# A transformer block on one core: QKV and output projections in 64-row tile pairs, one PSUM pool of six banks, the FFN gate applied to the sums, searched scheduler priorities

## The chip, the cores and the metric

The kernel runs on one core of a Trainium2 chip. The metric is the device time of one execution in microseconds (us); the "span" of a profile runs from the first to the last recorded instruction and is about 1.8 us shorter. The engines are named as the profile names them: PE (TensorE, matmuls), PEld (its weight loads, which overlap with PE), DVE (VectorE), ACT (ScalarE), POOL (GpSimd) and SP (SyncE, which here issues most of the transfers). A line number such as L614 is a line of the kernel that was profiled, so the same step has other numbers in the changed kernel. A "tile" of PE below is the part of the 128x128 array that a matmul uses: all 128 rows, or 64, or 28 to 32 of them, and all columns or 64 or 32 of them; the tile mode is this size. PSUM holds the sums that matmuls write; the kernel divides it into banks of 512 float32 columns. An eviction is the operation that reads a finished sum out of a bank, and only after it is the bank free again.

## The reference

One block with adaptive layer norm, for 2048 tokens of 448 numbers in bfloat16. The attention is local and dilated: each token looks at eight keys, 0, 2, ..., 14 positions back.

```python
# cut to what matters; S = 2048, D = 448, H = 16 heads of 28, F = 1792, dtype bfloat16
mod = silu(c) @ w_mod                       # six vectors of 448: sa, ca, ga, sb, cb, gb
h = layernorm(x) * (1 + ca) + sa
q, k, v = split(h @ wqkv)                   # wqkv: 448 x 1344
o = softmax(q . k[t - 0, 2, ..., 14] / sqrt(28)) @ v      # per head
x = x + ga * (o @ wo)
h = layernorm(x) * (1 + cb) + sb
gate, up = h @ W_gate, h @ W_up             # 448 x 1792 each
x = x + gb * ((relu(gate) * up) @ W_down)
```

The contraction over D = 448 matters here: it is three and a half times 128, and exactly seven times 64.

## The kernel before

The kernel hands every operation to a static scheduler in Python. It knows for each operation an engine (or several), an estimated duration, a priority and what it depends on. It orders the operations on each engine, assigns PSUM banks and buffers, and derives the semaphore waits. An order on an engine is therefore decided by priorities and by estimates, not by the order of the program text.

```python
class _Plan:
    def op(self, eng, cost, fn, r=(), w=(), prio=0, drain=0.0, dma=0, issue=450.0, mode=128, after=()):
        ...     # `mode` is the tile shape on PE: a change costs SWITCH in the plan's estimate;
        ...     # `after`: PE operations that this one must wait for with a semaphore

psF = es.enter_context(nc.psum_tensor("psF", [128, 4, 512], F32))
psL = es.enter_context(nc.psum_tensor("psL", [128, 2, 512], F32))
psM = es.enter_context(nc.psum_tensor("psM", [128, 2, 512], F32))
poolF = _Slots([psF[:, i, :] for i in range(4)])      # QK, V, gate/up
poolL = _Slots([psL])                                 # scores
poolM = _Slots([psM[:, i, :] for i in range(2)])      # denominators, attention sums, projection, down

def stage_qk(b, prio):                                # per block b of 512 tokens
    for g in range(4):
        for sec in range(2):                          # q, then k
            buf = _Buf(poolF)
            def mm(e, g=g, sec=sec, buf=buf):
                for k in range(4):                    # rows 448..511 are zeros
                    last = e.matmul(buf.at, Wqk[:, k, 512 * sec + 128 * g:512 * sec + 128 * g + 128],
                                    hT[:, k, KOFF + TB * b:KOFF + TB * b + TB], start=(k == 0), stop=(k == 3))
                return last
            ...   # evictions to qT (twice, with alternate heads zeroed) or kT

def stage_v(t, prio):                                 # per attention tile t of 114 tokens (18 tiles)
    ...
    for k in range(4):
        last = e.matmul(buf.at[0:nk, 0:D], hT[:, k, KOFF + k0:KOFF + k0 + nk], Wv[:, k, :],
                        start=(k == 0), stop=(k == 3))

def stage_y(j, prio, eprio):                          # output projection, 128 tokens, mode 128
    ...
    for g in range(4):                                # four groups of 4 heads x 32 rows (28 used)
        last = e.matmul(buf.at[:, 0:D], qT[:, g, s0:s0 + 128], wo_pad[:, g, :], start=(g == 0), stop=(g == 3))

def stage_gu(b, h2, prio, eprio):                     # gate and up side by side in 64-row tiles, mode 64
    ...
    for c in range(7):
        e.matmul(bufs[0].at, Wgu[0:64, c, 128*f:128*f+128], h2.at[0:64, kg, :], start=(c == 0), stop=(c == 6))
        e.matmul(bufs[1].at, Wgu[64:128, c, 128*f:128*f+128], h2.at[64:128, ku, :], start=(c == 0), stop=(c == 6))

# the gate gb (gbc[:, 1]) is multiplied into W_down, once:
for f in range(NF):                                   # NF = 14
    op(POOL, 1000, lambda e, f=f: e.tensor_tensor(Wd[:, f, :], Wd[:, f, :], gbc[:, 1, :], ALU.mult),
       r=[("Wd", f), ("gbc", 1)], w=[("Wds", f)], prio=900)
# ... so that a down projection ends with one addition:
op(DVE, 620, lambda e, ...: e.tensor_tensor(o.at, buf.at[:, 0:D], x_sb[:, t, :], ALU.add), ...)
```

The down projection runs in 64-row pairs in two of the four blocks (`DN64 = (1, 2)`) and in 128 rows in the others. Score matmuls use 64 rows; denominators and attention sums use all rows and 32 columns.

The softmax here doesn't subtract the row's maximum and nothing guards it: scores larger than these inputs give would overflow.

Of the kernel before, what the change touches and what calls it, by code (L numbers as in the profile page):

```python
# [5 lines left out]
ACT = mybir.ActivationFunctionType  # L6
# [19 lines left out]
DNP = (1350, 1550, 1750, 1950)  # L26
# [25 lines left out]
class _Plan:  # L52
# [3 lines left out]
    DMA_NS_PER_BYTE = 1.0 / 240.0  # L56
# [7 lines left out]
    def op(self, eng, cost, fn, r=(), w=(), prio=0, drain=0.0, dma=0, issue=450.0, mode=128, after=()):  # L64
# [22 lines left out]
        else:  # L87
            alts = [(e, float(c), f) for e, c, f in eng]
        self.ops.append(dict(id=oid, alts=alts, deps=deps, allocs=allocs, prio=prio,
                             drain=drain, dma=dma, issue=issue, mode=mode, after=list(after)))  # L90
# [7 lines left out]
    def schedule(self):  # L98
# [14 lines left out]
        mode = 128  # L113
        slack = {PE: 30.0 + self.SWITCH, ACTE: 60.0, DVE: 60.0, POOL: 60.0, SP: 60.0}
# [22 lines left out]
        for _ in range(n):  # L137
            cands = {e: [] for e in ENGINES}
            for oid in avail:
# [14 lines left out]
                for a, (e, c, f) in enumerate(o["alts"]):  # L154
# [10 lines left out]
                    st = max(free[e] + (self.SWITCH if e == PE and o["mode"] != mode else 0.0), rt)  # L165
                    if best is None or st + c < best[0] - 1e-6:
                        best = (st + c, st, a, e)
# [22 lines left out]
            if o["dma"]:  # L190
                free[e] = st + o["issue"]
                b0 = max(free[e], dma_free)
                dma_free = b0 + o["dma"] * self.DMA_NS_PER_BYTE
                finish[oid] = dma_free + self.DMA_FIXED
            else:
                free[e] = st + cost
                finish[oid] = free[e] + o["drain"]
            o["st"] = st
# [88 lines left out]
def bass_adaLN_cond__sliding_local_dilated__glu_gated_reglu__prompt_kernel(  # L287
# [15 lines left out]
    with ExitStack() as es:  # L303
# [51 lines left out]
        qsc = sb("qsc", [128, 2], F32)  # L355

        psF = es.enter_context(nc.psum_tensor("psF", [128, 4, 512], F32))
        psL = es.enter_context(nc.psum_tensor("psL", [128, 2, 512], F32))
        psM = es.enter_context(nc.psum_tensor("psM", [128, 2, 512], F32))
        poolF = _Slots([psF[:, i, :] for i in range(4)])  # L360
        poolL = _Slots([psL])
        poolM = _Slots([psM[:, i, :] for i in range(2)])
# [20 lines left out]
        op(DVE, 60, lambda e: e.memset(qsc[:], 0.0), w=["qsc"], prio=-15)  # L383
        for r in range(4):
# [4 lines left out]
        op(DVE, 500, lambda e: e.memset(hT[64:128, 3, KOFF:KOFF + 2 * TB], 0.0), w=["hT0"], prio=-13)  # L389
        op(DVE, 500, lambda e: e.memset(Wqk[64:128, 3, :], 0.0), w=["wqkz"], prio=-14)  # L390
        op(DVE, 250, lambda e: e.memset(Wv[64:128, 3, :], 0.0), w=["wvz"], prio=-13)
# [33 lines left out]
        def load_x(ta, tb, prio, eng=SP):  # L425
            load(x_sb[:, ta:tb, :], x2d[128 * ta:128 * tb, :].rearrange("(t p) d -> p t d", p=128),
                 [("x", t) for t in range(ta, tb)], 128 * (tb - ta) * D * 2, prio, eng=eng)

        wmod_v = w_mod.rearrange("(p k) n -> p k n", k=4)
        load(crow[:], c.rearrange("o (p k) -> (o p) k", k=4), ["crow"], 4096, -10)  # L430
        load_x(0, 2, -9)
        load_x(2, 4, -9, eng=ACTE)
        load(wmod[0:112, 0:2, 0:2 * D], wmod_v[:, 0:2, 0:2 * D], ["wmodA0"], D * D * 2, -8)
        load(wmod[0:112, 2:4, 0:2 * D], wmod_v[:, 2:4, 0:2 * D], ["wmodA1"], D * D * 2, -8)
        load(Wv[:, 0:3, :], A_wqkv[0:384, 2 * D:3 * D].rearrange("(k p) n -> p k n", p=128),
             [("wv", k) for k in range(3)], 384 * D * 2, -7)
        load(Wv[0:64, 3, :], A_wqkv[384:448, 2 * D:3 * D], [("wv", 3)], 64 * D * 2, -7)
        load(Wraw[:, 0:3, :], A_wqkv[0:384, 0:2 * D].rearrange("(k p) n -> p k n", p=128),
             [("wraw", k) for k in range(3)], 384 * 2 * D * 2, -7)
        load(Wraw[0:64, 3, :], A_wqkv[384:448, 0:2 * D], [("wraw", 3)], 64 * 2 * D * 2, -7)  # L440
# [13 lines left out]
        op(POOL, 900, lambda e: e.memset(Wqk_h[:, :, :, DH:32], 0.0), r=["wqkz"], w=["wqk0"], prio=-16)  # L454
        for k in range(4):
            for sec in range(2):
                op(DVE, 275, lambda e, k=k, sec=sec: e.tensor_copy(
                    Wqk_h[0:ROWS[k], k, 16 * sec:16 * sec + 16, 0:DH],
                    Wraw[0:ROWS[k], k, D * sec:D * sec + D].rearrange("p (h d) -> p h d", d=DH)),
                   r=[("wraw", k), "wqk0"], w=[("wqk", k, sec)], prio=1)  # L460
# [10 lines left out]
        def mod_cols(vecs, wname, col, prio):  # L471
            buf = _Buf(poolM)

            def mm(e, ks):
                last = None
                for k in ks:
                    for cc in range(4):
                        for vi, vec in enumerate(vecs):
                            M = ROWS[cc]
                            last = e.matmul(buf.at[0:M, 4 * vi + cc:4 * vi + cc + 1],  # L480
                                            wmod[0:112, k, D * vec + 128 * cc:D * vec + 128 * cc + M],
                                            silu[:, k:k + 1], start=(k == 0 and cc == 0 and vi == 0),
# [4 lines left out]
            for i in range(2):  # L487
                op(PE, 750, lambda e, i=i: mm(e, (2 * i, 2 * i + 1)), r=[wname + str(i), "silu"], w=[buf, ("mm", col, i)], prio=prio,
# [23 lines left out]
        def ln_stats(t, stt, mvt, tag, prio, extra=()):  # L512
            op(DVE, 600, lambda e: e.bn_stats(stt[:, t, :], x_sb[:, t, :]), r=[("x", t)] + list(extra),  # L513
               w=[(tag, "st", t)], prio=prio)
            op(DVE, 165, lambda e: e.bn_aggr(mvt[:, t, :], stt[:, t, :]), r=[(tag, "st", t)],
               w=[(tag, "mv", t)], prio=prio)

        def ln_rstd(t0, t1, mvt, lt, rt, nt, tag, prio):
# [5 lines left out]
            op(DVE, 90, lambda e: e.scalar_tensor_tensor(nt[:, t0:t1], mvt[:, t0:t1, 0], -1.0, rt[:, t0:t1],  # L524
# [4 lines left out]
        def ln_normalize(t, rt, nt, tag, prio, eng, extra=()):  # L529
# [3 lines left out]
            op(eng, 390 if eng == DVE else 720, f, r=[("x", t), (tag, "rstd", t), (tag, "nmr", t)], w=[buf] + list(extra),  # L533
               prio=prio)
# [6 lines left out]
        def ln_affine(dst, deps, w, col, rows, cc, prio):  # L541
# [4 lines left out]
            op(POOL, 850, f, r=deps + [("mod", col), ("mod", col + 4)], w=w, prio=prio)  # L546


# [398 lines left out]
```

## Time and profile before

| | before |
|---|---|
| median of the first three runs, known before the prediction | 237.11 us (234.69 to 238.84) |
| median of four, with the one beside the changed kernel | 236.38 us |
| medians in three later sets of 7, 7 and 9 runs on other chips | 235.11, 235.04, 234.87 us |
| the profiled run: time, span, mean granted clock | 234.78 us, 233.0 us, 0.997 |

Below, everything read from profiles is compared with profiles.

The head of the profile page gives the span, and per engine busy time, share and number of instructions:

```profile
span 233.0 us, 5200 instructions
PE 223.9 (96%) x2216; PEld 104.9 (45%) x2216; DVE 148.3 (64%) x291; ACT 124.4 (53%) x212; POOL 60.8 (26%) x83
```

PE is busy for 96% of the span, and the next engine is far behind. The page's groups of instructions show the work in question: line, engine, operation, output<-inputs, tile of the array, size, count | busy us, mean ns | idle before, and what ended it:

```profile
L614 PE MATMUL psF<-hT,Wqk 128*128 128x512 bf16 x128 | 29.3, 380 | 1.4 <-DVE kT L632 1.4
...
L647 PE MATMUL psF<-Wv,hT 128*128 128x448 bf16 (+1 forms) x72 | 15.2, 353 | 1.6 <-ACT hT L575 1.6
...
L860 POOL TENSOR_TENSOR Wd<-Wd,gbc 128x448 bf16<-128x448 bf16 x14 | 14.0, 1031 | 6.3 <-DVE gbc L508 6.3
...
L742 PE MATMUL psM<-wo_pad,qT 128*128 128x448 bf16 x64 | 14.9, 355 | 0.0
```

A mean of 380 ns for a matmul is not its cost: matmuls overlap in the records, and what counts is the distance from one start to the next. The next lines are from the timeline of PE (start, duration, line, operation, count of a group):

```profile
12.60 2.44 PE L647 MATMUL psF<-Wv,hT 128*128 128x448 bf16 x12 [0.89 <-ACT hT L575]
14.88 7.07 PE L614 MATMUL psF<-hT,Wqk 128*128 128x512 bf16 x32
...
118.49 0.38 PE L780 MATMUL psF<-h2T,Wgu 64*128 64x512 bf16 x1
118.49 0.38 PE L782 MATMUL psF<-h2T,Wgu 64*128 64x512 bf16 x1
118.80 0.93 PE L742 MATMUL psM<-wo_pad,qT 128*128 128x448 bf16 x4
119.66 0.38 PE L710 MATMUL psM<-EA,ones 128*32 128x456 bf16 x4
119.97 0.22 PE L682 MATMUL psL<-qT,kT 64*128 64x114 bf16 x2
```

Thirty-two 512-column matmuls take 7.07 us, 0.216 us each, and the two of a 64-row pair start together and also take 0.216 us. Four projection matmuls of 448 columns should take 4 x 0.189 = 0.76 us, but the next work starts 0.86 us after them. The extra 0.1 us appears at each change of the tile mode shown here: gate/up (64 rows) to projection (128 rows), 0.31 us from start to start instead of 0.216; projection to denominators (32 columns), 0.86 instead of 0.76. Few other delays exist. The list of PE's waits shows them (what waited, releaser, total us, times, longest); the line left out is the warm-up before any real work:

```profile
PE psF L647 <- ACT hT L575: 1.6, 2, 0.9
PE psF L614 <- DVE kT L632: 1.4, 1, 1.4
...
PE psL L682 <- ACT EA L694: 0.5, 1, 0.5
```

The end is short: the last matmul's record ends at 229.21 us, then comes one eviction, here from the timeline of DVE, and the last output transfer.

```profile
229.25 0.62 DVE L838 TENSOR_TENSOR o_sb<-psF,x_sb 128x448 bf16<-128x448 f32 x1 [2.03 <-PE psF L831]
```

### The profile page before, as it was taken

The numbers are of one execution on the slowest core, as the hardware profiler recorded it, in microseconds if no ns is written. First come the engines' busy times: TensorE is split into PE (matmuls) and PEld (weight loads), VectorE is DVE, ScalarE is ACT, GpSimd is POOL, SyncE is SP. The second block draws the span as 40 slices with busy tenths as digits, with TensorE's granted clock in tenths as the row PEclk, the third lists the DMA queues.
The fourth block names the chain that finished last, engine by engine and source line by source line (L and its number), as shares of the span: only waits on it lengthen the run. The fifth ranks groups of instructions, "written<-read, shape, count | busy, mean of one in ns | idle before, by whom it ended". The sixth has DMA issues, their size and how long they took to land. (4 is left out here: it accounts for less than half of the span.)

```text
span 233.0 us, 5200 instructions
## 1 busy us (share of the span) xinstructions
PE 223.9 (96%) x2216; PEld 104.9 (45%) x2216; DVE 148.3 (64%) x291; ACT 124.4 (53%) x212; POOL 60.8 (26%) x83
## 2 busy tenths in 40 slices
PE   7989899999997999999999999999999999999993
PEld 2645445644443444444444444344444444444451
DVE  7787987797457677876878897843543343343331
ACT  2268996896776767876568778323233223323100
POOL 6404672339990000203602035135000000000000
PEclk9999999999999999999999999999999999999998
DMA  6999999604200000021201230022000010010111
GB/s 183 289 263 243 184 234 226 219 1 48 45 0 0 3 3 0 3 45 32 57 23 31 17 48 1 3 67 46 0 33 10 0 42 0 3 39 3 39 41 41
DMA packets 18992, 14.94 MB, mean 64 GB/s; under 512 B 9496, under 2 KB 17624, under 8 KB 18968
## 3 DMA queue, kind: packets, MB, share of 16 engines
q1 hardware_dynamic: 18696, 14.37, 26.8%
q8 instruction: 17, 0.28, 0.5%
q10 hardware_dynamic: 272, 0.23, 0.3%
q14 instruction: 7, 0.06, 0.1%
HBM read 10.67 MB, written 1.84 MB: 54 GB/s over the span
## 5 line engine op out<-in xcount | busy, mean ns | idle before, releaser
L780 PE MATMUL psF<-h2T,Wgu 64*128 64x512 bf16 x392 | 90.9, 376 | 0.2 <-DVE bigR L790 0.2
L782 PE MATMUL psF<-h2T,Wgu 64*128 64x512 bf16 x392 | 90.9, 376 | 0.0
L790 DVE TENSOR_TENSOR bigR<-psF,g_sb 128x512 bf16<-128x512 f32 x56 | 38.6, 689 | 42.6 <-ACT g_sb L788 42.0
L788 ACT ACTIVATE g_sb<-psF 128x512 bf16<-128x512 f32 x56 | 33.4, 596 | 56.7 <-PE psF L782 56.7
L780 PEld LDWEIGHTS psF<-h2T,Wgu 64*128 64x128 bf16 x392 | 35.4, 94 | 41.3 <-DVE bigR L790 0.9
L531 POOL TENSOR_SCALAR hb<-x_sb,rstd,nmr 128x448 bf16<-128x448 bf16 x28 | 22.1, 799 | 79.1 <-DVE nmr L524 72.7
L694 ACT ACTIVATE EA<-psL 128x912 bf16<-128x912 f32 (+1 forms) x36 | 33.1, 920 | 5.0 <-PE psL L682 4.7
L782 PEld LDWEIGHTS psF<-h2T,Wgu 64*128 64x128 bf16 x392 | 35.4, 94 | 0.0
L614 PE MATMUL psF<-hT,Wqk 128*128 128x512 bf16 x128 | 29.3, 380 | 1.4 <-DVE kT L632 1.4
L700 DVE TENSOR_TENSOR EA<-EA,maskA 128x912 bf16<-128x912 bf16 (+1 forms) x36 | 23.8, 676 | 3.3 <-ACT EA L694 2.8
L808 PE MATMUL psM<-Wd,bigR 64*128 64x448 bf16 x224 | 23.5, 349 | 0.0
L513 DVE BATCH_NORM_STATS2 st<-x_sb 128x6 f32<-128x448 bf16 x32 | 19.6, 613 | 0.8 <-DMA x_sb<-in_A_x_dram 0.3
L614 PEld LDWEIGHTS psF<-hT,Wqk 128*128 128x128 bf16 x128 | 12.0, 98 | 15.9 <-DVE kT L632 1.9
L647 PE MATMUL psF<-Wv,hT 128*128 128x448 bf16 (+1 forms) x72 | 15.2, 353 | 1.6 <-ACT hT L575 1.6
L544 POOL TENSOR_SCALAR h2T<-h2T,modc 128x512 bf16<-128x512 bf16 (+1 forms) x16 | 13.3, 842 | 10.5 <-DMA h2T<-hb 10.5
L808 PEld LDWEIGHTS psM<-Wd,bigR 64*128 64x128 bf16 x224 | 10.9, 94 | 11.0
L860 POOL TENSOR_TENSOR Wd<-Wd,gbc 128x448 bf16<-128x448 bf16 x14 | 14.0, 1031 | 6.3 <-DVE gbc L508 6.3
L731 DVE TENSOR_TENSOR qT<-psM,lnD 128x456 bf16<-128x456 f32 (+1 forms) x18 | 11.3, 629 | 6.0 <-PE psM L721 4.4
L742 PE MATMUL psM<-wo_pad,qT 128*128 128x448 bf16 x64 | 14.9, 355 | 0.0
L727 ACT ACTIVATE lnD<-psM 128x456 f32<-128x456 f32 (+1 forms) x18 | 9.9, 548 | 8.3 <-PE psM L710 8.3
L682 PE MATMUL psL<-qT,kT 64*128 64x114 bf16 (+1 forms) x144 | 11.8, 216 | 0.5 <-ACT EA L694 0.5
L622 ACT ACTIVATE qT<-psF,qsc 128x512 bf16<-128x512 f32 x13 | 8.9, 688 | 5.4 <-PE psF L614 5.3
(83 smaller groups left out, 239.8 us busy)
## 6 DMA issues: line engine op xcount, KB each, us to landing
out_dram<-o_sb SPq DMA_DIRECT2D x16, 112.0 KB, 1.7
Wd<-in_B_W_down_dram SPq DMA_DIRECT2D x1, 1568.0 KB, 25.6
x_sb<-in_A_x_dram SPq DMA_DIRECT2D x3, 448.0 KB, 10.0
Wgu<-in_B_W_gate_dram SPq DMA_DIRECT2D x3, 448.0 KB, 17.5
Wgu<-in_B_W_up_dram SPq DMA_DIRECT2D x3, 448.0 KB, 18.8
bigR<-in_w_mod_dram SPq DMA_DIRECT2D x3, 392.0 KB, 6.6
bigR<-in_w_mod_dram SPq DMA_DIRECT2D x1, 1176.0 KB, 15.8
bigR<-in_A_wqkv_dram SPq DMA_DIRECT2D x1, 672.0 KB, 8.1
```

The source lines that it names most:

```text
L513: op(DVE, 600, lambda e: e.bn_stats(stt[:, t, :], x_sb[:, t, :]), r=[("x", t)] + list(extra), w=[(tag, "st", t)], prio=prio)
L531: f = lambda e: e.tensor_scalar(buf.at[:, 0:D], x_sb[:, t, :], rt[:, t:t + 1], nt[:, t:t + 1], ALU.mult, ALU.add)
L614: last = e.matmul(buf.at, Wqk[:, k, 512 * sec + 128 * g:512 * sec + 128 * g + 128], hT[:, k, KOFF + TB * b:KOFF + TB * b + TB], start=(k = ...
L647: last = e.matmul(buf.at[0:nk, 0:D], hT[:, k, KOFF + k0:KOFF + k0 + nk], Wv[:, k, :], start=(k == 0), stop=(k == 3))
L694: return e.activation(dst, src, ACT.Exp)
L700: return e.tensor_tensor(d, d, msk[0:nk, None, 0:nq].to_broadcast([nk, 8, nq]), ALU.mult)
L742: last = e.matmul(buf.at[:, 0:D], qT[:, g, s0:s0 + 128], wo_pad[:, g, :], start=(g == 0), stop=(g == 3))
L780: e.matmul(bufs[0].at, Wgu[0:64, c, 128 * f:128 * f + 128], h2.at[0:64, kg, :], start=(c == 0), stop=(c == 6))
L782: last = e.matmul(bufs[1].at, Wgu[64:128, c, 128 * f:128 * f + 128], h2.at[64:128, ku, :], start=(c == 0), stop=(c == 6))
L788: op(ACTE, _act(TB), lambda e, gs=gs, gb=bufs[0]: e.activation(gs.at, gb.at, ACT.Relu), r=[bufs[0]], w=[gs], prio=eprio)
L790: op(DVE, _dve(TB), lambda e, gs=gs, ub=bufs[1], f=f: e.tensor_tensor(hh.at[:, f, :], ub.at, gs.at, ALU.mult), r=[bufs[1], gs] + ([hh] if ...
L808: last = e.matmul(bufs[i].at[:, 0:D], hh.at[rows[i], f, 128 * (j + i):128 * (j + i) + 128], Wd[rows[i], f, :], start=(phase == 0 and f == ...
```

## The change

The intent is to shorten the work of PE. A 448-row contraction in 128-row passes needs four passes for one output, the last of them half empty. In 64-row tiles two outputs can be computed at once, in seven pairs of passes for two outputs instead of eight passes. For that, output 0 first takes rows 0 to 63 of each chunk while output 1 takes rows 64 to 127; then they exchange the halves. The exchange needs a wait of PE on its own semaphore. The Trainium skill states why, in "TensorEngine Tiling (Array Packing)", Gotcha 1: different row tiles may not access the same PSUM bank at once, and software must see to it. The last chunk is loaded from rows 320 to 447, so that both halves hold data, and the zero padding goes.

The same diff also changes the output projection to pairs (its contraction is padded to 512 rows, so no pass is saved), joins the two PSUM pools, moves the gate from the weights to the sums, and replaces the hand-set priorities by numbers from a search. Smaller parts: the first layer norm in halves, another order of the first transfers, 28-row score tiles for the first five attention tiles, modulation matmuls always 128 columns wide, swaps of activations by DMA in three blocks, and a rule that keeps certain DVE operations apart from POOL operations in the plan.

```diff
+PR = { "ln1": [537, 334, 2613, 2241], "qk": [711, 1230, 2349, 2507], ... }     # cut
+T32 = 5
+SWAP_DVE = (0,)
-        psF = es.enter_context(nc.psum_tensor("psF", [128, 4, 512], F32))
+        psF = es.enter_context(nc.psum_tensor("psF", [128, 6, 512], F32))
         psL = es.enter_context(nc.psum_tensor("psL", [128, 2, 512], F32))
-        psM = es.enter_context(nc.psum_tensor("psM", [128, 2, 512], F32))
-        poolF = _Slots([psF[:, i, :] for i in range(4)])
+        poolF = _Slots([psF[:, i, :] for i in range(6)])
-        poolM = _Slots([psM[:, i, :] for i in range(2)])
+        poolM = poolF
 # stage_qk
-                        for k in range(4):
-                            last = e.matmul(buf.at, Wqk[:, k, 512 * sec + 128 * g:512 * sec + 128 * g + 128], hT[:, k, ...],
-                                            start=(k == 0), stop=(k == 3))
+                bufs = [_Buf(poolF), _Buf(poolF)]
+                prev = None
+                for phase in range(2):
+                    def mm(e, g=g, bufs=bufs, phase=phase):
+                        for n in range(4 - phase):
+                            for sec in range(2):
+                                k = 3 if phase and n == 2 and sec == 0 else n
+                                h0 = 64 * (sec ^ phase)
+                                c0 = 512 * sec + 128 * g
+                                last = e.matmul(bufs[sec].at, Wqk[h0:h0 + 64, k, c0:c0 + 128], hT[h0:h0 + 64, k, ...],
+                                                start=(phase == 0 and n == 0), stop=(phase == 1 and n == 2))
+                        return last
+                    prev = op(PE, (4 - phase) * _mm(TB), mm, mode=64, ..., after=[prev] if phase else [])
 # stage_v likewise, for attention tiles t and t + 1; stage_y, for token tiles j and j + 1:
-                for g in range(4):
-                    last = e.matmul(buf.at[:, 0:D], qT[:, g, s0:s0 + 128], wo_pad[:, g, :], start=(g == 0), stop=(g == 3))
+                    for g in range(4):
+                        for i in range(2):
+                            h0 = 64 * (i ^ phase)
+                            s0 = 128 * (j + i)
+                            last = e.matmul(bufs[i].at[:, 0:D], qT[h0:h0 + 64, g, s0:s0 + 128], wo_pad[h0:h0 + 64, g, :],
+                                            start=(phase == 0 and g == 0), stop=(phase == 1 and g == 3))
 # the gate
-        for f in range(NF):
-            op(POOL, 1000, lambda e, f=f: e.tensor_tensor(Wd[:, f, :], Wd[:, f, :], gbc[:, 1, :], ALU.mult), ..., prio=900)
+        def stage_out(t, buf, eng, eprio):            # eng: POOL, but DVE in the last block
+            o = _Buf(o_slots)
+            op(DVE, 620, lambda e: e.tensor_tensor(o.at, buf.at[:, 0:D], gbc[:, 1, :], ALU.mult), ...)
+            op(eng, 400 if eng == DVE else 1030, lambda e: e.tensor_tensor(o.at, o.at, x_sb[:, t, :], ALU.add), ...)
+            op(SP, 0, lambda e: e.dma_start(out2d[128 * t:128 * t + 128, :], o.at), ...)
 # the modulation columns
-                            M = ROWS[cc]               # 128, 128, 128, 64
-                            last = e.matmul(buf.at[0:M, ...], wmod[0:112, k, D * vec + 128 * cc:D * vec + 128 * cc + M], ...)
+                            c0 = D * vec + (320 if col == 0 and cc == 3 else 128 * cc)
+                            last = e.matmul(buf.at[:, ...], wmod[0:112, k, c0:c0 + 128], ...)
 # the first transfers
-        load(crow[:], c..., ["crow"], 4096, -10)
-        load_x(0, 2, -9)
-        load_x(2, 4, -9, eng=ACTE)
+        load_x(0, 2, -9, eng=ACTE)
+        load(crow[:], c..., ["crow"], 4096, -9, eng=ACTE)
+        ...      # w_mod in three parts on SP, load_x(2, 4) after the first of them
```

The cuts leave out index expressions, dependency lists, the evictions, the layer-norm code and the rest of the load list.

## The prediction

> **What bounds the kernel now.** TensorE. The table of engines gives PE 223.9 us busy of a 233.0 us span (96%), against 148.3 for DVE, 124.4 for ACT and 60.8 for POOL. The chain of waits is almost wholly PE from 144 to 229.25 us; then come a 0.62 us eviction and the last output transfer. In the PE timeline, real work starts at 12.6 us (before it: warm-up matmuls and the first layer norm); idle is 0.89 + 0.69 + 0.47 + 0.25 + 1.42 = about 3.7 us. So time comes from PE work, PE's overhead between instructions, and the start.
>
> **PE work removed.** In the timeline, 512-column matmuls follow each other every 0.216 us, 448-column ones every 0.189 us, and the 392 gate/up pairs of 64 rows run two at once at 0.216 a pair. A contraction of 448 rows is 4 passes of 128 (the last half empty), or 7 pair-passes of 64 for two outputs. QK: 128 matmuls become 112 pairs, -16 x 0.216 = -3.45 us. V: 72 become 63 pairs, -1.7 us. The output projection has 512 padded rows: no gain. Together -5.15 us.
>
> **Mode switches.** The Trainium skill, "TensorEngine Tiling (Array Packing)", Key Properties, says that changing the tiling mode drains TensorE. The trace agrees: between output projection (128 rows), scores (64 rows) and column-tiled steps I read gaps of about 0.09 us. By the instruction order, such switches fall from 106 to about 66, because QK, V and projection now share the mode of gate/up: estimated -3.5 us.
>
> **Added on PE.** Each pair must exchange row halves, with a wait on PE's own semaphore (same page, Gotcha 1: row tiles can't use one bank at once). There are 33 such waits, but only about 11 stand directly behind their own first half; elsewhere other work fills them. A matmul's record ends 0.16 us after its issue slot, so I estimate 0.2 us each: +2.2 us.
>
> **Other engines.** Scaling W_down on POOL goes (14 x 1.03 us); 16 adds come, of about 1 us on POOL (0.4 on DVE in the last block). Both are off the chain, except for the tail: +0.4 us. Four q evictions (0.69 us) and three pairs of DVE swaps (1.45 + 0.69 us) go. Nine score tiles instead of 5.5 now come before gate/up starts, which loads ACT more there (it was 80 to 90% busy). I expect no new bound; this is the weakest point.
>
> **Start and idle.** With layer norm in halves, the first V pair needs only two x tiles: about -1.0 us. Six shared banks and new priorities: of 3.7 us idle, -1.2 us.
>
> **Sum.** -5.15 - 3.5 + 2.2 + 0.4 - 1.0 - 1.2 = about -8.2 us of span: about 225 us, 3.5%. From the median of 237.1 that is **228.5 us, range 223.5 to 234**. Faster by over 2%: 0.83; within 2%: 0.14; slower: 0.03.
>
> **Right if:** QK and V pairs run at 0.216 and 0.189 us; PE busy falls to about 216 us; the first V matmul comes near 11.5 us; PE idle is about 2.5 us; the last matmul ends near 221 us, with a tail 0.4 us longer; gate/up starts near 74 us with more attention done.
>
> **Wrong if:** the half-exchange waits cost 0.4 us or more; ACT or DVE become the bound before gate/up (PE idle in 20 to 75 us above 5 us); the DMA swap of activations arrives late and gate/up waits; output buffers, held longer by the POOL add, stop the down projection; or switches return under 2 us (then 230 to 232).

## The result

| | before | after |
|---|---|---|
| median (range), four runs each on one chip | 236.38 us (234.69 to 238.84) | 224.02 us (223.89 to 224.10) |
| profiled run: time, span, clock | 234.78, 233.0 us, 0.997 | 224.05, 222.2 us, 1.0 |

The changed kernel is correct. The ratio is 0.9499, with a 95% interval of 0.9438 to 0.9561. Ratios here are the mean time of one kernel's fast runs over that of the other's of the same rounds, so they are not quite the ratio of the medians quoted. When the changed kernel was run again on another chip (the run called control), the ratio was 0.9562, with 0.9546 to 0.9578; there the kernel before had less scatter. Executions over 1.5% slower than the fastest of the same kernel are left out of the means. (Of the runs before, the one of 238.84 us counts as slow and is left out of the ratio.) So the gain is 10 to 12 us; between the two profiles it is 10.8 us.

The head of the page and the groups after:

```profile
span 222.2 us, 5740 instructions
PE 212.7 (96%) x2452; PEld 102.7 (46%) x2452; DVE 143.3 (65%) x299; ACT 119.5 (54%) x210; POOL 49.1 (22%) x73
```

```profile
L681 PE MATMUL psF<-hT,Wqk 64*128 64x512 bf16 x224 | 27.9, 377 | 0.5 <-ACT kT L703 0.2
...
L893 POOL TENSOR_TENSOR o_sb<-o_sb,x_sb 128x448 bf16<-128x448 bf16 x12 | 12.2, 1031 | 26.3 <-DVE o_sb L891 26.3
...
L832 PE MATMUL psF<-wo_pad,qT 64*128 64x448 bf16 x128 | 14.6, 350 | 0.6 <-DVE qT L818 0.5
L724 PE MATMUL psF<-Wv,hT 64*128 64x448 bf16 x126 | 14.2, 352 | 0.3
```

PE is still 96% busy, of a span that is 10.8 us shorter: the bound has not moved, it has shrunk. The counts answer to the intent: 224 matmuls of QK are 112 pairs in place of 128, and 126 of V are 63 pairs in place of 72; 128 of the projection are 64 pairs in place of 64. The timeline of PE after:

```profile
11.58 3.30 PE L724 MATMUL psF<-Wv,hT 64*128 64x448 bf16 x28
14.72 3.19 PE L681 MATMUL psF<-hT,Wqk 64*128 64x512 bf16 x28
...
86.19 0.38 PE L875 MATMUL psF<-h2T,Wgu 64*128 64x512 bf16 x1
...
86.40 0.92 PE L832 MATMUL psF<-wo_pad,qT 64*128 64x448 bf16 x8
87.16 0.21 PE L763 MATMUL psL<-qT,kT 64*128 64x114 bf16 x2
...
87.39 0.93 PE L832 MATMUL psF<-wo_pad,qT 64*128 64x448 bf16 x8
88.16 0.38 PE L877 MATMUL psF<-h2T,Wgu 64*128 64x512 bf16 x1
```

Three things can be read here. From gate/up to the projection the distance is now 0.21 us: no gap, since the mode is the same. The first half of this projection pair takes its 0.76 us, scores come in between, and the second half follows without a wait: the exchange was hidden. At 11.58, however, 28 matmuls of V are 14 pairs and should take 14 x 0.189 = 2.65 us; the next work starts 3.14 us later. These are two V pairs whose halves stand directly behind each other, and two exchanges cost 0.49 us together, with the mode unchanged to QK. The profile's list of PE's waits does not show these gaps.

PE's waits after the start, from the list after (the first line belongs to the modulation matmuls, before the first V matmul):

```profile
PE psF L507 <- DVE silu L493: 1.7, 1, 1.7
...
PE psF L832 <- DVE qT L818: 0.5, 1, 0.5
```

The end, from the timeline of DVE, now has the two gate operations, the last matmul's record ending at 217.86:

```profile
217.89 0.62 DVE L891 TENSOR_TENSOR o_sb<-psF,gbc 128x448 bf16<-128x448 f32 x1 [1.53 <-PE psF L930]
218.55 0.39 DVE L893 TENSOR_TENSOR o_sb<-o_sb,x_sb 128x448 bf16<-128x448 bf16 x1
```

**The sum on PE.** I took the start of every matmul from both traces and split the time from the first V matmul to the last matmul's issue ("the PE stretch" below) into three parts: the number of passes times their rate (0.2158 us for 512 columns, 0.1892 for 448), gaps where the tile mode changes, and everything else that lies between starts.

| term, us | before | after | difference | predicted |
|---|---|---|---|---|
| passes at full rate | 199.41 | 194.28 | -5.13 | -5.15 |
| gaps at mode changes | 12.3 (113 changes) | 6.8 (65) | -5.5 | -3.5 |
| exchanges directly behind each other | 0 | 2.25 (10 gaps of 0.220 to 0.229) | +2.25 | +2.2 |
| idle: waits for other engines | 3.6 | 1.5 | -2.1 | -1.2 |
| rest | | | +0.2 | |
| **PE stretch** | 216.26 | 205.92 | -10.34 | -7.65 |
| start: first V matmul at | 12.60 | 11.58 | -1.0 | -1.0 |
| tail: last matmul's end to the end | 3.8 | 4.4 | +0.6 | +0.4 |
| **span** | 233.0 | 222.2 | -10.8 | -8.2 |

This is an accounting, in which the rate and the counts are measured, but the attribution of each gap is my reading. The split depends on where a pass is taken to end: a recount from the same two traces, which lets each pass end at its rate after its own start, gives 0.098 us for a mode change without a wait, so -4.8 us for mode changes and -2.6 us for idle. The counts of mode changes, the ten exchange gaps and the sum stay as in the table. The experiments test it.

### The profile page after: what moved, and what is told of

It reads as the page before. It is cut to its first block, busy times and chain, and to the rows that moved or that the text cites. A ratio compares the mean times of both kernels' runs of the same rounds, so it can differ in the third digit from the quotient of the medians.

```text
span 222.2 us, 5740 instructions
## 1 busy us (share of the span) xinstructions
PE 212.7 (96%) x2452; PEld 102.7 (46%) x2452; DVE 143.3 (65%) x299; ACT 119.5 (54%) x210; POOL 49.1 (22%) x73
## 4 chain that ended last, share of the span: by engine, by line
PE 87%; DVE 4%; ACT 3%; DMA 3%; issue 1%
PE psF L875 29%; PE psF L681 10%; PE psF L930 10%; PE psF L912 10%; PE psF L877 9%; PE psF L724 6%; PE psF L832 6%; PE psL L763 3%; DMA crow<-in_c_dram 3%; PE psF L796 2%; PE psF L808 1%; PE psF L619 1%; ACT EA L776 1%; DVE qT L696 1%; DVE EA L782 1%
## 5 line engine op out<-in xcount | busy, mean ns | idle before, releaser
L681 PE MATMUL psF<-hT,Wqk 64*128 64x512 bf16 x224 | 27.9, 377 | 0.5 <-ACT kT L703 0.2
L891 DVE TENSOR_TENSOR o_sb<-psF,gbc 128x448 bf16<-128x448 f32 x16 | 9.7, 622 | 22.7 <-PE psF L930 13.2
L912 PE MATMUL psF<-Wd,bigR 64*128 64x448 bf16 x224 | 22.5, 349 | 0.0
L930 PE MATMUL psF<-Wd,bigR 128*128 128x448 bf16 x112 | 21.5, 353 | 0.0
L893 POOL TENSOR_TENSOR o_sb<-o_sb,x_sb 128x448 bf16<-128x448 bf16 x12 | 12.2, 1031 | 26.3 <-DVE o_sb L891 26.3
L930 PEld LDWEIGHTS psF<-Wd,bigR 128*128 128x128 bf16 x112 | 10.8, 98 | 10.4 <-issue 0.4
L912 PEld LDWEIGHTS psF<-Wd,bigR 64*128 64x128 bf16 x224 | 10.8, 94 | 9.9
L832 PE MATMUL psF<-wo_pad,qT 64*128 64x448 bf16 x128 | 14.6, 350 | 0.6 <-DVE qT L818 0.5
L724 PE MATMUL psF<-Wv,hT 64*128 64x448 bf16 x126 | 14.2, 352 | 0.3
L818 DVE TENSOR_TENSOR qT<-psF,lnD 128x456 bf16<-128x456 f32 (+1 forms) x18 | 11.3, 627 | 2.2 <-ACT lnD L816 2.1
```

The source lines that it names most:

```text
L681: last = e.matmul(bufs[sec].at, Wqk[h0:h0 + 64, k, c0:c0 + 128], hT[h0:h0 + 64, k, KOFF + TB * b:KOFF + TB * b + TB], start=(phase == 0 an ...
L724: last = e.matmul(bufs[i].at[0:nk, 0:D], hT[h0:h0 + 64, k, KOFF + k0:KOFF + k0 + nk], Wv[h0:h0 + 64, k, :], start=(phase == 0 and n == 0), ...
L832: last = e.matmul(bufs[i].at[:, 0:D], qT[h0:h0 + 64, g, s0:s0 + 128], wo_pad[h0:h0 + 64, g, :], start=(phase == 0 and g == 0), stop=(phase ...
L912: last = e.matmul(bufs[i].at[:, 0:D], hh.at[rows[i], f, 128 * (j + i):128 * (j + i) + 128], Wd[rows[i], f, :], start=(phase == 0 and f == ...
L930: last = e.matmul(buf.at[:, 0:D], hh.at[:, f, 128 * j:128 * j + 128], Wd[:, f, :], start=(f == 0), stop=(f == NF - 1))
```

## The experiments

Twelve kernels ran, in three sets, each set on one chip beside the kernel before (medians in 7, 7 and 9 runs on other chips: 235.11, 235.04, 234.87 us). "Correct" means that the output agreed with the reference. The letters in the quoted expectations name the theories that are opposed in that quotation.

### 1. The projection in 128 rows again (y128)

The projection is the purest test of the mode changes, because its pair saves no pass. The order of instructions on PE stays the same; each half of the pair just becomes one whole output.

```diff
                     last = None
+                    s0 = 128 * (j + phase)
                     for g in range(4):
-                        for i in range(2):
-                            h0 = 64 * (i ^ phase)
-                            s0 = 128 * (j + i)
-                            last = e.matmul(bufs[i].at[:, 0:D], qT[h0:h0 + 64, g, s0:s0 + 128], wo_pad[h0:h0 + 64, g, :],
-                                            start=(phase == 0 and g == 0), stop=(phase == 1 and g == 3))
+                        last = e.matmul(bufs[phase].at[:, 0:D], qT[:, g, s0:s0 + 128], wo_pad[:, g, :],
+                                        start=(g == 0), stop=(g == 3))
```

> The changed kernel with the same instruction order, but each output projection runs over all 128 rows again: the same 64 passes of 448 columns, only in another tiling mode, so PE changes mode 88 times instead of 66. Theory A (PE's own stream sets the time; a mode change costs the 0.107 us read between bursts): 22 x 0.107 = +2.4 us, so about 226.4 us against 224.0. Rival B (the gain of the change is in priorities and banks, PE has slack): under +0.5 us.

Measured: correct, median 227.48 us (226.56 to 228.80), ratio 0.9691 to the kernel before. In the profile, the PE stretch grew from 205.92 to 208.33 us, +2.41, and the mode changes from 65 to 87: 0.11 us for each of 22 more, if all of it is theirs. (The wait of PE on its own semaphore between the two halves was kept in this edit.) The timeline of PE shows it at the same place as above:

```profile
86.82 0.38 PE L875 MATMUL psF<-h2T,Wgu 64*128 64x512 bf16 x1
87.13 0.93 PE L830 MATMUL psF<-wo_pad,qT 128*128 128x448 bf16 x4
87.99 0.23 PE L763 MATMUL psL<-qT,kT 64*128 64x114 bf16 x2
...
88.30 0.93 PE L830 MATMUL psF<-wo_pad,qT 128*128 128x448 bf16 x4
89.16 0.39 PE L873 MATMUL psF<-h2T,Wgu 64*128 64x512 bf16 x1
```

From the last gate/up before to the first after it is 2.34 us here, and 1.97 us in the changed kernel (86.19 to 88.16): four mode changes at 0.09 us. The work in passes is identical. So it is shown that the pairs of the projection, which save no pass, are worth 2 to 2.4 us through the mode alone (22 changes at 0.09 to 0.11 us). The profiled run is the fastest of its four; the median lies 2.9 us above control (224.58, on another chip) and 3.5 us above the first set of the change, which is 0.5 to 1.1 us more than the mode changes explain.

### 2. QK and V in 128 rows again (qkv128)

```diff
-                        for n in range(4 - phase):
-                            for sec in range(2):
-                                k = 3 if phase and n == 2 and sec == 0 else n
-                                h0 = 64 * (sec ^ phase)
-                                ...
+                        c0 = 512 * phase + 128 * g
+                        for k in range(4):
+                            last = e.matmul(bufs[phase].at, Wqk[:, k, c0:c0 + 128], hT[:, k, ...], start=(k == 0), stop=(k == 3))
+        # V likewise; rows 0 to 63 of the last weight chunk, which would count twice, are zeros
```

> The changed kernel with the same plan, but Q, K and V run over 128 rows again (four passes for one output instead of seven for two; the doubled rows of the last chunk are zeroed). Theory A: +16 x 0.216 + 9 x 0.189 = +5.15 us of passes and 9 more mode changes = +1.0 us, so about +6.1 us, 230.1 us. Rival B: these stages lie where DVE and ACT are over 85% busy, so PE would only wait less: under +3 us.

Measured: correct; three runs of 230.46 to 230.59 us, with 230.1 expected; ratio 0.9802. Against the changed kernel (224.02, or 224.58 in its repetition) that is 6.0 to 6.5 us. One thing limits the reading: the edit kept the waits of PE on its own semaphore (`after=[prev]`), although whole outputs need none. What they cost is seen in the trace of the next kernel. A fourth execution, the profiled one, took 786.17 us and is set aside as slow: the 512-column gate/up matmuls in it took 1,101 ns on average where 376 is usual, and three quarters of the distances between 512-column matmuls were 0.84 us in place of 0.216, so PE ran at about a quarter of its usual rate, while the operations of DVE and ACT took their usual time. The clock is given as 1.0, but this trace holds no clock record at all. It did not happen again, and no run explains it. So there is no usable trace for this kernel, only its time.

### 3. Both (all128)

The edits of 1 and 2 together: what is left of the change is pools, gate, start, small tiles, priorities, and the 33 self-waits of the pairs, which the edits kept.

> Both of these: Q, K, V and output projection over 128 rows, all else of the change kept. Theory A: +5.15 us of passes and 24 more mode changes x 0.107 = +2.6 us, together about +7.7 us, 231.7 us, and what is left of the gain (about 3 to 4 us against the kernel before) belongs to start, idle time, banks and priorities. Rival B: under +4 us, most of the gain left.

Measured: correct, median 232.35 us (232.15 to 233.67), ratio 0.9892 (0.9849 to 0.9935). The PE stretch is 213.53 us, +7.6 against the changed kernel, with +7.7 expected; mode changes rise to 89. The kernel is still 1.1% faster than the one before, about 2.6 us. This is not yet what the rest of the change is worth, because of the self-waits. The first V burst shows them in the timeline of PE:

```profile
12.38 3.65 PE L725 MATMUL psF<-Wv,hT 128*128 128x448 bf16 x16
15.87 3.62 PE L685 MATMUL psF<-hT,Wqk 128*128 128x512 bf16 x16
```

Sixteen passes should take 3.03 us, and the next work starts after 3.49. The starts of the single matmuls have ten gaps of 0.22 us in this trace, at the same ten places as in the changed kernel, though no halves are exchanged here: the gap belongs to the wait. A kernel in 128 rows needs no such wait, so an estimate from these ten gaps takes 2.2 us off all128. Then the pairs are worth about 5.4 us net (7.6 - 2.2), and the rest of the change about 4.8 us (2.6 + 2.2): each about half of the gain. This kernel without the waits was not run.

### 4. No exchange (noswap)

Each output keeps its half of the rows, so the result is wrong (relative error 0.034), while passes, tile sizes and order stay the same. The wait on PE's own semaphore is dropped because its reason is gone: no bank is now touched by two row tiles.

```diff
-                                h0 = 64 * (sec ^ phase)
+                                h0 = 64 * sec            # in QK; likewise 64 * i in V and in the projection
 # semaphores: the 33 self-waits of these stages are left out
```

> Wrong on purpose: the changed kernel with identical instruction order, but the second half of each QKV and projection pair keeps its row half, so the banks aren't exchanged and PE needn't wait for itself (33 waits gone). Results are wrong, times count. Theory A: the exchange costs the about 2.0 us of gaps that I read inside V, QK and projection bursts, so about 222.0 us. Rival: other work hides them, or the gaps are something else: 223.7 or more.

Measured: median 222.98 us (222.32 to 223.20), ratio 0.9477. The PE stretch is 203.42 us, 2.5 less, and all ten inner gaps are gone. The first V burst shows it in the timeline of PE:

```profile
12.35 2.83 PE L724 MATMUL psF<-Wv,hT 64*128 64x448 bf16 x28
15.01 1.25 PE L681 MATMUL psF<-hT,Wqk 64*128 64x512 bf16 x10
```

From start to start 2.66 us, where it was 3.14, and 2.65 is the rate. The whole time fell by 1.0 us only, not 2.0, because in the profiled run the first V matmul came 0.77 us later. In the runs with the changed start that moment is not constant: 11.12 (control), 11.58, 11.59, 12.35, 12.38 us, following the moment at which x lands. So the exchanges' cost of 2.3 to 2.5 us on PE is shown by the stretch; as a time it is blurred by the start.

### 5. The hand-set priorities (oldprio)

The table of searched priorities is filled with the numbers of the kernel before.

```diff
-    "ln1": [537, 334, 2613, 2241],
-    "qk": [711, 1230, 2349, 2507],
+    "ln1": [0, 30, 145, 250],
+    "qk": [50, 142, 300, 400],
     ...      # all thirteen lists
```

> The changed kernel with the hand-set priorities of the kernel before in place of the searched ones; everything else kept. Its instruction order has 78 mode changes instead of 66. Theory A (PE's stream is the clock; searched priorities gain by fewer mode changes and less idle): 12 x 0.107 = +1.3 us and idle back toward the 3.6 us of before (+2.1), so about 227.4 us. Rival C (the searched priorities are the larger part of the gain, above 5 us): 229 or more. Rival D (they don't matter): 224.5 or less.

Measured: correct, median 226.82 us (226.43 to 226.99), ratio 0.9651, with 227.4 expected. Mode changes rise from 65 to 77; the gaps at them, together with waits that fall there, from 7.2 to 9.5 us (by the recount named above); the PE stretch rises by 2.28. The search is worth about 2.3 to 2.8 us, and what it found is chiefly an order with fewer mode changes and less waiting.

### 6. Two pools of four and two banks (pool42)

```diff
-        poolF = _Slots([psF[:, i, :] for i in range(6)])
-        poolM = poolF
+        poolF = _Slots([psF[:, i, :] for i in range(4)])
+        poolM = _Slots([psF[:, i, :] for i in (4, 5)])
```

> The changed kernel with its six banks split again, four for the QKV and gate/up tiles and two for the rest, searched priorities kept. Its order has 87 mode changes instead of 66. Theory A: +21 x 0.107 = +2.2 us, plus some idle (a pair needs both of the two small banks): 226 to 228 us. Rival: banks don't matter once PE is the bound: under 224.5.

Measured: correct, median 247.27 us (246.38 to 251.60), ratio 1.0506. This is 20 us outside what was expected, and slower than the kernel before. The profiled run was the slowest (251.60 us, counted as slow, at a mean granted clock of 0.957); the fast ones show 0.968 to 0.974, so the lowered clock is in all of them. PE's waits in the profiled run:

```profile
PE psL L763 <- ACT EA L776: 3.3, 4, 1.1
...
PE psF L912 <- DVE x_sb L838: 2.1, 1, 2.1
```

The listed waits alone do not make 23 us. In this run the granted clock is halved in five stretches, of 3.41 us each except one of 6.83, 20.5 us in all. At half the rate that is an estimated 10 us lost. The stretch of 3.41 us before each of them has PE busy for 1.1 to 1.9 us. The waits open gaps, and the gaps cost once more through the clock.

### 7. Is it the searched order that can't live with two banks? (pool42old)

The rivals were: the searched priorities had been found for six banks and fit no other pool; or the pair itself needs both small banks, whatever the order. The kernel combines the edits of 5 and 6.

> Banks split four and two, and hand-set priorities. The split with searched priorities took 247 us. Theory I (the priorities were searched for six shared banks; with others the split costs only its mode changes and some idle): 227 to 230 us. Rival J (structural: projection pairs hold both small banks at once, which starves attention): 235 or more, with PE waiting for DVE and ACT between 40 and 90 us again.

Measured: correct, median 249.70 us (248.95 to 253.72), ratio 1.0619. The first rival needed 227 to 230 us and falls. With hand-set priorities, too, the changed kernel does not work with four and two banks. The window from 150 to 180 us, in the view of busy time per window (window, its length, then per engine busy us and instructions for PE, PEld, DVE, ACT and POOL, granted clock, DMA share, GB/s):

```profile
150.00:180.00 30.00, 20.84 (x186) 7.79 (x184) 14.48 (x34) 7.34 (x17) 10.92 (x15) 0.72 0.24 51
```

This is the profile of its slowest run (253.72 us); the others have mean clocks of 0.966 to 0.968. PE is busy for 20.84 of 30 us at a mean clock of 0.72; the changed kernel is busy for all of it at 1.00 (its line follows in experiment 8). A projection pair or a down-projection pair takes both small banks at once and holds them until its second half has been evicted. That denominators and attention sums wait behind it fits the waits listed, on DVE's additions to x and on the attention's results, but which step holds the bank longest was not separated. Shown is the consequence: the changed kernel needs the larger pool. That the pairs are what needs it is likely, since the kernel before lived with four and two banks, but it was not tested: no run undoes the pairs on the split pools.

### 8. The gate back on W_down (gatew)

```diff
-            op(DVE, 620, lambda e: e.tensor_tensor(o.at, buf.at[:, 0:D], gbc[:, 1, :], ALU.mult), ...)
-            op(eng, ..., lambda e: e.tensor_tensor(o.at, o.at, x_sb[:, t, :], ALU.add), ...)
+            op(DVE, 620, lambda e: e.tensor_tensor(o.at, buf.at[:, 0:D], x_sb[:, t, :], ALU.add), ...)
+        for f in range(NF):
+            op(POOL, 1040, lambda e, f=f: e.tensor_tensor(Wd[:, f, :], Wd[:, f, :], gbc[:, 1, :], ALU.mult),
+               r=[("Wd", f), ("gbc", 1)], w=[("Wds", f)], prio=3000)
```

> The changed kernel with the gate multiplied into W_down again (14 POOL operations of about 1 us, one add per output tile instead of multiply and add). Theory A (both off the chain, but for the tail): 4 more mode changes in its order = +0.4 us, tail shorter by the second operation (0.4 us) = about 224.0, between 223.3 and 224.8. Rival E (the POOL work of W_down delays the second layer norm and so gate/up): 226 or more, with PE idle before gate/up starts.

Measured: correct, median 233.54 us (232.71 to 234.34), ratio 0.9934. About 224.0 was expected: a miss of 9.5 us, for 14 us of POOL work on an engine that is idle three quarters of the time. The windows of this kernel:

```profile
40.00:72.00 32.00, 29.29 (x443) 15.04 (x442) 27.49 (x57) 25.84 (x45) 17.59 (x20) 1.00 0.22 58
...
74.66:78.07 3.41, 1.61 (x26) 0.70 (x22) 3.34 (x8) 2.78 (x4) 0.00 (x0) 1.00 0.00 0
78.07:81.48 3.41, 2.50 (x50) 1.48 (x52) 3.28 (x8) 2.42 (x6) 0.18 (x1) 0.50 0.00 0
81.48:84.90 3.42, 3.42 (x24) 1.43 (x22) 1.65 (x3) 1.74 (x4) 1.25 (x2) 0.50 0.27 43
```

The same view of the changed kernel:

```profile
40.00:72.00 32.00, 31.12 (x465) 15.92 (x464) 27.67 (x57) 28.45 (x49) 5.75 (x8) 1.00 0.22 59
72.00:90.00 18.00, 18.00 (x250) 8.79 (x248) 14.59 (x26) 13.23 (x24) 1.43 (x2) 1.00 0.10 17
...
150.00:180.00 30.00, 30.00 (x294) 14.07 (x292) 15.32 (x29) 9.36 (x18) 7.83 (x10) 1.00 0.20 47
```

The POOL operations ran from 46.5 to 64.5 us, in the stretch where attention, layer norm and evictions compete; ACT did 2.6 us less work there, PE 1.8 us less. The attention came late, PE waited up to 1.74 us at once for exponentials, from 76.6 us on, and was busy for 1.61 us of the 3.41 before 78.07. Then the clock was halved for 6.83 us: the timeline has gate/up pairs every 0.43 us from 81.65 on, in place of every 0.216. Together the PE stretch is 8.3 us longer.

### 9. The same work, later (gatelate)

The same edit, with one more dependency: the POOL operations may start only after the second layer norm of block 0.

```diff
-               r=[("Wd", f), ("gbc", 1)], w=[("Wds", f)], prio=3000)
+               r=[("Wd", f), ("gbc", 1), (h2s[0], 5)], w=[("Wds", f)], prio=3000)
```

> The gate multiplied into W_down as in the run that lost 9.5 us, but the 14 POOL operations may start only after the first block's second layer norm is done (about 73 us), so they stay out of the busy stretch and end before the first down projection (about 98 us). Theory E (what costs is the POOL work between 46 and 66 us, while it holds up masks and layer norm): within 1 us of the change, 223.3 to 225.0 us. Rival H (the gate on the weights costs wherever it is put, or the loss is a searched plan that no longer fits): 228 or more.

Measured: correct, median 224.25 us (223.98 to 225.51), ratio 0.9557 to the kernel before; the changed kernel itself had 224.58 and 0.9562 in the same set. Its window from 72 to 90 us:

```profile
72.00:90.00 18.00, 17.79 (x234) 8.28 (x232) 13.74 (x24) 12.89 (x24) 14.36 (x16) 1.00 0.15 15
```

The 14 us of POOL work stand here, and PE is busy for 17.79 of 18 us all the same. So the gate on the sums does not save 9 us. The same 14 operations cost 9.5 us at 46 to 64 us, and nothing measurable 25 us later (71.3 to 90.4 us). They even shorten the tail by 0.42 us (3.95 in place of 4.37), which was the only price seen of moving the gate; the profiled run, this kernel's slowest, spent 1.9 us more on PE elsewhere, most of it in one stop within a burst of scores, from 43.2 us on (1.24 us, for which the profile names no releaser). What exactly the early operations hold up, whether the masks on DVE that the plan keeps apart from POOL work, or POOL's own layer-norm steps queued behind them, was not separated. Nor was the plan itself: with POOL taken early, the scheduler also divided other work anew (DVE evicts vaug 10 and kT 8 times, in place of 8 and 7 in the changed kernel and in gatelate), so part of the loss may lie in the order that it made.

### 10. The first transfers (xfirst, xfirst2, with control)

The first V matmul waits for x tiles 0 and 1. In the changed kernel x tiles 0 and 1 stand first on the ACT queue and the small c behind them; on the SP queue a part of w_mod stands before x tiles 2 and 3. The first try exchanged the first two transfers of each queue:

```diff
+        for q in (SP, ACTE):
+            first = P.order[q]
+            i, j = [n for n, oid in enumerate(first) if P.ops[oid]["dma"]][:2]
+            first[i], first[j] = first[j], first[i]
```

> The changed kernel, same plan, but at the start the loads of x and c are issued ahead of the first part of w_mod (two swaps in the queues). In the trace of the change x lands late (layer norm starts at 5.5 us; before: 4.05), and in three of its relatives the first V started at 11.6 to 12.4 us with it. Theory F (the landing of x is the start's chain): layer norm at about 4.2 us, first V near 10.6 us, time about 223.0 us. Rival G (w_mod's landing is the chain): no gain, 224.0 or more.

Measured: correct, median 224.43 us (224.02 to 224.85), ratio 0.9547: no gain. The trace says why: x tiles 2 and 3, now first on SP, landed 2.9 us after issue, but tiles 0 and 1, second on ACT, 4.2 us after theirs, and the first statistics began at 5.47 us as before (5.49). The wrong tiles had been hurried. The second try also exchanges which x tiles go through which queue: tiles 0 and 1 first on SP; c first and tiles 2 and 3 second on ACT.

```diff
+        a = next(i for i in order[ACTE] if ops[i]["dma"])            # x tiles 0-1
+        b = [i for i in order[SP] if ops[i]["dma"]][1]               # x tiles 2-3
+        ...                                                          # exchanged between the queues,
+        ops[a]["eng"], ops[b]["eng"] = SP, ACTE                      # then the first two of each as above
```

> The changed kernel once more, as it is, on the chip of the next three: 224.0 us as before on another chip, 223.6 to 224.6; its first V at 11.6 to 12.4 us. If runs vary, it is the landing of x at the start.

> As the failed start experiment, but the x tiles that layer norm needs first (0 and 1) are now the first transfer of the sync queue, c the first of the ACT queue, x tiles 2 and 3 second there. In the failed one the first transfer of the sync queue landed at 3.6 us and the second of the ACT queue at 5.45 us, and layer norm waited for the latter. Theory F (landing of x is the chain): layer norm of tile 0 at about 4 us, first V near 10.6 us, 0.7 to 1.2 us faster than the control. Rival G (w_mod, or the order of ACT, is the chain): less than 0.3 us.

Measured: the changed kernel again (control), median 224.58 us (223.61 to 224.80, six runs), ratio 0.9562; xfirst2, correct, median 222.98 us (222.47 to 223.23, four runs), ratio 0.9489 (0.9470 to 0.9508). The means are 224.46 and 222.91, which makes xfirst2 1.5 us faster, a little more than expected. Its times and those of control do not overlap. The timeline of DVE, first of control and then of xfirst2:

```profile
5.07 0.63 DVE L538 BATCH_NORM_STATS2 st<-x_sb 128x6 f32<-128x448 bf16 x1 [2.37 <-DMA x_sb<-in_A_x_dram]
```

```profile
3.69 0.63 DVE L547 BATCH_NORM_STATS2 st<-x_sb 128x6 f32<-128x448 bf16 x1 [0.99 <-DMA x_sb<-in_A_x_dram]
```

The statistics start 1.38 us earlier; the first V matmul comes at 10.71 us in place of 11.12 in these two profiled runs, and the PE stretch is the same to the hundredth, 205.94 us. The list of transfers within the first 9 us shows what else moved (output<-source, queue, count, size, median us from issue to landing), first control, then xfirst2:

```profile
x_sb<-in_A_x_dram ACTq DMA_DIRECT2D x1, 224.0 KB, 4.3
...
crow<-in_c_dram ACTq DMA_DIRECT2D x1, 0.9 KB, 4.9
```

```profile
x_sb<-in_A_x_dram SPq DMA_DIRECT2D x1, 224.0 KB, 2.9
...
crow<-in_c_dram ACTq DMA_DIRECT2D x1, 0.9 KB, 2.4
```

The profiled run of control was its fastest, so these two traces differ by less than the means: 0.4 us of span, which is the 0.41 us of the first V matmul. Where the rest of the 1.5 us between the means lies, no kept trace shows. The Trainium skill, "DMA: Bandwidth & Descriptors", section "Issuing engines are not separate DMA queues", says that transfers started by different engines run on the same 16 DMA engines and interleave. The trace fits that: first on the ACT queue, x still shared the engines with the w_mod part that SP had issued, and took 4.3 us; first on SP, with only 0.9 KB first on the other queue, it took 2.9. Whether the queue itself has a part in it was not separated. This is the fastest version; it beats both kernels.

## Why the prediction was right

The result lies inside the range, near its lower end, and on the side predicted as most likely. The predicted 228.5 us is 4.5 us above the measured 224.0. Of this, about 2.1 us come from the starting point, since the prediction subtracted from a median of 237.1 that later runs put at 235.0; the rest are terms that were too small, 2.6 us in the span.

- **What bounds the kernel: right.** PE was 96% busy before and is after; the change paid through PE's own time. PE busy fell to 212.7 us rather than 216, and the last matmul ended at 217.9 rather than near 221.
- **Passes removed, -5.15 us: right**, -5.13. The pairs run at the predicted 0.216 and 0.189 us. It was the safest term, since gate/up already ran in this form in the trace before.
- **Mode switches, -3.5 us: right in kind, too small.** This is the mis-sized step: "such switches fall from 106 to about 66", at "about 0.09 us". The traces count 113 and 65, at 0.10 to 0.11 us: 48 fewer, -4.8 to -5.5 us. The seven missed ones before all lie at the modulation matmuls, which changed column width for the last chunk (64 in place of 128). A group of 16 of them lasted 0.83 us before and 0.55 after, since the changed kernel always takes 128 columns. That a change of mode itself costs was tested by y128, and not only argued.
- **Added exchanges, +2.2 us: right**, +2.25 by the gaps and 2.5 by their removal (noswap). Of 33 exchanges ten stand directly behind each other and cost 0.22 to 0.23 us; the 23 others cost nothing that can be seen. So the pairs alone, with passes, half of the saved mode changes and exchanges, are worth about 5.4 us: half of the gain.
- **Other engines, +0.4 us in the tail: right for the change itself**, +0.6 measured. But "off the chain" was taken as a property of the operations. Experiment 8 shows that scaling W_down, which cost little in the order before (all of PE's waits together were 3.6 us), would have cost 9.5 us in the new kernel if it was planned as early as it can run; experiment 9 shows that it would have cost nothing if it ran later. The prediction was spared this by luck, since the change moves that work away.
- **More attention before gate/up: no new bound, as expected.** Gate/up starts at 71.4 us (74.4 before), with nine score tiles done in place of 5.5. PE's waits over the whole stretch fell to 1.5 us.
- **Start, -1.0 us: right** in the profiled run, though that moment scatters by over 1 us between runs of the same start code.
- **Idle, -1.2 us: too small**, -2.1 to -2.6. The prediction gave this to the six banks and the priorities together. The priorities are worth 2.3 to 2.8 us including their share of the mode changes. The six banks can't be given a sum of this kind: without them the changed kernel takes 247 to 250 us, more than the kernel before. They are a condition of the gain, and the prediction did not see that; its number does not suffer, because the change has them.

The pairs, the priorities, the pools, the gate and the order of the first transfers were changed back or varied in the new kernel, the pairs with their self-waits kept; the start in halves, the small score tiles and the DMA swaps were not tried alone.

## What to carry to other kernels

When PE bounds a kernel, split its time into passes at their rate, changes of tile mode, exchanges and waits, from the starts of the matmuls. Give neighbouring work the same tile mode even where that saves no pass (about 0.1 us for each change, 2 to 2.4 us here), put other work between the two halves of an exchanged pair, and make sure that the pool has banks for two outputs at once. When a pair is undone as a test, take out its wait too. Judge work on an idle engine by when it runs, and put the transfer that the first work waits for first where no other transfer shares the engines with it.

## What the Trainium skill lacked or had wrong

- "TensorEngine Tiling (Array Packing)", Key Properties: it says that changing the tiling mode drains TensorE, and gives no cost. Here it is 0.09 to 0.11 us for each change, by how the end of a pass is counted, over 113 and 65 of them; the PE stretch of y128, with 22 more, is 2.41 us longer. A switch of the column width from 128 to 64 counts too (16 modulation matmuls: 0.83 us, or 0.55 with one width).
- The same page, Gotcha 1: it asks for synchronisation between row tiles on one bank, and gives neither a cost nor a way to hide it. Here an exchange costs 0.220 to 0.229 us when the second half stands directly behind the first (10 cases), and nothing to be seen with other work between (23 cases); the same wait without an exchange costs as much (0.22 us, ten times in all128). It names the pressure on banks but not that it can turn a gain into a loss: the same kernel takes 224 us with six shared banks and 247 to 250 us with four and two.
- "TensorE: Matmul & The Clock Gate", "Why this matters for your kernels": it warns of idle gaps above about 3 us. Here the clock was halved for 6.83 us from 78.07 us on in gatew, when the longest gap had lasted 1.45 us (of 1.74 in all); PE was busy for 1.61 of the preceding 3.41 us (in pool42 once for 1.88 of 3.41, at 40.34 to 43.75 us). So shorter gaps are enough. No threshold comes out of these runs: the clock stayed up after 1.77 of 3.41 us in xfirst2 (215.23 to 218.64 us) and was halved after 2.84 of 3.41 us in pool42old (35.76 to 39.17 us). Another section of the page, "A second HAM failure mode: psum-queue depth-cycling", does tell of frequent short idle times that make the clock swing, without a length. The stretches of 3.41 us agree with the page's window of 3413 ns.
- The same page, "Seeing it yourself", mentions a clock that stayed at a quarter for over 50 us, and gives no cause. The execution of 786.17 us, with 512-column matmuls mostly 0.84 us apart in place of 0.216 over the whole run, looks like such a case; its trace holds no clock record, so no run here settles it.
